# The remainder of v in an attention kernel: from one SBUF copy in one operation instead of from two PSUM banks in two

## The chip, the cores and the metric

One core of a Trainium2 chip runs the whole program. The metric is the device time of one execution in microseconds (us). The core has five engines that run their own instruction lists in order and wait for each other by semaphores: TensorE (PE; its weight loads are shown apart as PEld), VectorE (DVE), ScalarE (ACT), GpSimd (POOL) and SyncE (SP), which issues the DMAs. SBUF is the working memory; PSUM is the memory that matmuls write, in banks of 128 x 512 numbers of 32 bits.

## What is computed

A transformer block on x of 2048 tokens x 1024 features, modulated by a condition c. Cut to what matters here:

```python
# half A: attention with 32 heads of 32, in 4 segments of 512 tokens, with a memory (M, z)
h = layernorm(x) * (1 + ca) + sa
q, k, v = h @ wq, h @ wk, h @ wv              # per head, per segment s
p = softmax(q_s k_s^T * scale + causal mask)
a_dot = p @ v_s
a_mem = (phi(q_s) @ M) / (phi(q_s) @ z + 1e-6)
o = g * a_mem + (1 - g) * a_dot               # g = sigmoid(beta) per head
M, z = M + phi(k_s)^T v_s, z + sum(phi(k_s))
x = x + ga * (o @ wo)
# half B: token-mixing MLP
x = x + gb * (w2 gelu(w1 layernorm(x)^T * ... + b1) + b2)^T
```

The kernel reaches the precision of 32-bit numbers by splitting operands into parts of fewer bits. For v, the parts are three bf16 numbers: vp part 1 is v rounded to bf16, r1 = v - part 1 is the remainder, part 2 is r1 rounded to bf16, part 3 is r1 - part 2. The change is about where r1 is computed from.

## The kernel before, in words

**Stages.** Modulation and the first segment's normed tokens (to about 60 us of the run), attention (about 60 to 1085 us, its end overlapping the output projection "po"), and the MLP (L862 and its helpers) to the end.

**Attention.** Heads go in 8 groups of 4, segments in two passes of two; a round t of 32 is one group and one segment. A count n goes through the 128 heads of all rounds, and each step n does `scores(n)` (L475 to L490), `maxima(n+3)` (L440, L441, L447 to L450), `values(n-1)` (L504 to L521) and one of four pieces of `project` for the round two ahead:

- pieces 0 and 1 project k and v of half the segment's tokens into one bank of PSUM, tag "pj", of which there are two (nps, L196). ScalarE then copies from the bank: k to `k32` (L358), v to `v32` (L359, 32-bit, in SBUF), v rounded to bf16 to the first part of `vp` (L364). VectorE subtracts that part from the bank's v, into half of `r1` (L365 and L366).
- piece 2 transposes k into the next "pj" bank (kps, L372), splits it (L123 on ScalarE, L126 on VectorE), projects q into the one after (qps, L204), and splits that. It also makes phi(q) and phi(k) and starts the DMAs that stack the operands ("sk") of the scores.
- piece 3 rounds r1 into the second part of vp (L399, ScalarE), subtracts into the third (L400, VectorE), and reads and updates the memory (rd L412, up L422).

The two "pj" banks are taken in turn: first half of k and v, second half, kps, qps, and then the next round's first half. A bank is taken again when all readers of its tile have finished. `v32` and `r1` are single buffers, `vp` has three.

**Order.** Each engine runs its list in order. The lists are not simply the program's order: the framework plans them when the program is built, from its own durations and the dependencies of the tiles, so that on TensorE pieces of a projection stand between scores, maxima and values of other heads. `issue_after` adds a few orders by hand, none of them at the changed line.

**Other work in the stage.** GpSimd masks the exponentials (L486) and makes the second part of p (L490, two operations of 128 x 640 per head, reading and writing SBUF); VectorE takes the maxima (L441), the sums over parts (L507 to L511) and splits of weights (L126).

Of the kernel before, what the change touches and what calls it, by code (L numbers as in the profile page):

```python
# [12 lines left out]
ALU = mybir.AluOpType  # L13
# [32 lines left out]
def attention_and_mlp(ctx, tc, x, wq, wkv, wo, beta, w1, b1, w2, b2, c, wm_a, wm_b, out):  # L46
    nc = tc.nc
    V, A, G, T, SY = nc.vector, nc.scalar, nc.gpsimd, nc.tensor, nc.sync
# [17 lines left out]
    a = par.__enter__()  # L66
# [9 lines left out]
    def bank(tag, bufs, name):  # L76
        return psum.tile([P, 512], F32, tag=tag, bufs=bufs, name=name)
# [41 lines left out]
    def split(dst, src, hi_eng, lo_eng):  # L119

        hi, lo = dst[:, 0], dst[:, 1]
        if hi_eng is A:
            last_hi[0] = A.copy(hi, src)  # L123
        else:
            hi_eng.tensor_copy(hi, src)
        lo_eng.tensor_tensor(lo, src, hi.bitcast(F32), op=ALU.subtract)  # L126
# [62 lines left out]
    def kv_chunk(w, h, half, k, ps):  # L189
        wt = w["v", k // 2]  # L190
        o = 256 * (k % 2)
        n = 6 * k
        for i, j in ((0, 0), (0, 1), (1, 0)):
            for aa in range(2):
                tt = 2 * half + aa
                T.matmul(ps[:, aa], h[:, j, 128 * tt:128 * tt + 128], wt[:, i, o:o + 256],  # L196
                         start=(n == 0), stop=(n >= 6 * NK - 2), skip_group_check=True)
                n += 1

    def q_chunk(w, h, k, ps):  # L200
        wt = w["q", k // 4]
        o = 128 * (k % 4)
        for n, (i, j) in enumerate(((0, 0), (0, 1), (1, 0))):
            T.matmul(ps, wt[:, i, o:o + 128], h[:, j], start=(k + n == 0), stop=(3 * k + n == 3 * NK - 1))  # L204

    def two_tiles(ps):
        return ps.rearrange("p (a n) -> p a n", a=2)
# [51 lines left out]
    for i in range(2):  # L259
        ps = bank("pj", 2, f"scps{i}")  # L260
# [67 lines left out]
    def stack(t, h):  # L328


        sk = st[t]["sk", h] = skt[t % 2][h]
        skf = sk.bitcast(F32)
        src = st[t]["sg"].bitcast(F32)[32 * h:32 * h + 32]
        SY.dma_start(skf[0:32], src[:, 0:3:2])
        SY.dma_start(skf[32:64], src[:, 0:4:3])
        last_sk[t, h] = SY.dma_start(skf[64:96], src[:, 1:3])

    def project(t, piece):
        pr, g, seg = its[t]
        if piece == 0:  # L340
            st[t] = {}
        w = W[pr, g]
        hp = [hpages[seg, ct] for ct in range(NK)]
        d = st[t]
        if piece in (0, 1):
            if piece == 0:
                d["k32"] = pj.tile([P, 4, 128], F32, tag="k32", bufs=1, name=f"k32_{t}")
                d["v32"] = pj.tile([P, 4, 132], F32, tag="v32", bufs=1, name=f"v32_{t}")
                G.memset(d["v32"][:, :, 128:132], 1.0)
            half = piece  # L350
            k32, v32 = d["k32"], d["v32"]
            if t:
                ps = two_tiles(bank("pj", 2, f"nps{t}_{half}"))
                for k in range(NK):
                    kv_chunk(w, hp[k], half, k, ps)
            else:
                ps = two_tiles(first[half])
            A.copy(k32[:, 2 * half:2 * half + 2], ps[:, :, 0:128])  # L358
            A.copy(v32[:, 2 * half:2 * half + 2, 0:128], ps[:, :, 128:256])  # L359
            if half == 0:  # L360
                d["vp"] = b.tile([P, 4, 4, NV], BF16, tag="vp", bufs=3, name=f"vp{t}")
                G.memset(d["vp"][:, :, :, 0:1], 1.0)
                d["r1"] = pj.tile([P, 4, 4, 32], F32, tag="r1", bufs=1, name=f"r1_{t}")
            A.copy(d["vp"][:, 2 * half:2 * half + 2, :, 1:33], ps[:, :, 128:256].rearrange("p a (h e) -> p a h e", h=4))  # L364
            V.tensor_tensor(d["r1"][:, 2 * half:2 * half + 2], ps[:, :, 128:256].rearrange("p a (h e) -> p a h e", h=4),  # L365
                            d["vp"][:, 2 * half:2 * half + 2, :, 1:33], op=ALU.subtract)  # L366
        elif piece == 2:
            k32 = d["k32"]
            d["sg"] = sg = pj.tile([P, 4, L], F32R, tag="sg", bufs=1, name=f"sg{t}")
            ps = bank("pj", 2, f"kps{t}")  # L370
            for i in range(4):
                T.transpose(ps[:, 128 * i:128 * i + 128], k32[:, i], ident)  # L372
            split(sg[:, 2:4], ps, A, V)
            if t:
                ps = bank("pj", 2, f"qps{t}")
                for k in range(NK):
                    q_chunk(w, hp[k], k, ps)
            else:
                ps = first[2]
            split(sg[:, 0:2], ps, A, V)  # L380
            if seg:
                r = pj.tile([P, L], F32, tag="tmp", bufs=2, name=f"rq{t}")
                A.activation(r, ps, AF.Relu, scale=-1.0)
                A.activation(r, r, AF.Exp, scale=-1.0)
                d["pq"] = pj.tile([P, L], F32, tag="pq", bufs=1, name=f"pq{t}")
                V.scalar_tensor_tensor(d["pq"], ps, 0.0, r, op0=ALU.max, op1=ALU.add)
            if seg < 3:
                r = pj.tile([P, L], F32, tag="tmp", bufs=2, name=f"rk{t}")
                kf = k32.rearrange("p a n -> p (a n)")
                A.activation(r, kf, AF.Relu, scale=-1.0)  # L390
                A.activation(r, r, AF.Exp, scale=-1.0)
                d["pk"] = pj.tile([P, 4, 128], F32, tag="pk", bufs=1, name=f"pk{t}")
                V.scalar_tensor_tensor(d["pk"].rearrange("p a n -> p (a n)"), kf, 0.0, r, op0=ALU.max, op1=ALU.add)
            for h in range(3):
                stack(t, h)
        else:
            stack(t, 3)
            vp, r1 = d["vp"], d["r1"]
            A.copy(vp[:, :, :, 33:65], r1)  # L399
            V.tensor_tensor(vp[:, :, :, 65:97], r1, vp[:, :, :, 33:65], op=ALU.subtract)  # L400
            memory(t)

    def memory(t):
        pr, g, seg = its[t]
        d = st[t]
        d["am"] = am = b.tile([P, 4, 128], F32, tag="am", bufs=3, name=f"am{t}")
        if seg:
            for half in range(2):
                ps = bank("ms", 1, f"rd{t}_{half}")[:, 0:264].rearrange("p (a n) -> p a n", a=2)
                for aa in range(2):  # L410
                    i = 2 * half + aa
                    T.matmul(ps[:, aa], d["pq"][:, 128 * i:128 * i + 128], MZ[:, g], start=True, stop=True)  # L412
                rd = b.tile([P, 2, 4], F32, tag="rd", bufs=2, name=f"rdd{t}_{half}")
                V.tensor_scalar_add(rd, ps[:, :, 128:132], 1e-6)
                V.reciprocal(rd, rd)
                V.tensor_tensor(am[:, 2 * half:2 * half + 2].rearrange("p a (h e) -> p a h e", h=4),
                                ps[:, :, 0:128].rearrange("p a (h e) -> p a h e", h=4),
                                rd.unsqueeze(3).to_broadcast([P, 2, 4, 32]), op=ALU.mult)
        if seg < 3:
            ps = bank("ms", 1, f"up{t}")  # L420
            for i in range(4):
                T.matmul(ps[:, 0:132], d["pk"][:, i], d["v32"][:, i], start=(i == 0), stop=(i == 3))  # L422
            if seg == 0:
                V.tensor_tensor(MZ[:, g], ps[:, 0:132], bdg[:, g], op=ALU.mult)
            else:
                tm = b.tile([P, 132], F32, tag="tm", bufs=1, name=f"tm{t}")
                V.tensor_tensor(tm, ps[:, 0:132], bdg[:, g], op=ALU.mult)
                G.tensor_tensor(MZ[:, g], MZ[:, g], tm, op=ALU.add)
# [139 lines left out]
    def spread(dst, i):  # L568
        SY.dma_start(dst, bass.AP(tensor=modd.tensor, offset=modd.offset + D * i, ap=[[0, P], [1, D]]))

    project(0, 0)
    project(0, 1)
    with tc.issue_after(last_wm.ins):
        seg_load(1)
    project(0, 2)
    project(0, 3)
    seg_chunks(1, 0, 8)
# [505 lines left out]
```

## Time and profile before

| what | value |
|---|---|
| runs | 2258.55, 2255.84, 2258.07 us; median 2258.07 |
| profiled execution, first to last instruction (its span) | 2252.7 us |
| median of the runs above that span | 5.4 us |
| mean granted clock of TensorE | 0.993 |
| L364 (ScalarE's copy of v's first part), 64 times | 350 / 385 / 430 ns (min / median / max) |
| L399 (ScalarE, second part), 32 times | 612 / 634 / 702 ns |
| bytes moved by DMA | 423.06 MB, mean 188 GB/s |

The profile is of one execution, whose whole time is not given beside its span; what lies before the first and behind the last instruction is not in it. Line numbers (L365) are those of the kernel printed above. A row of a group gives its engine, operation, the tiles it writes and reads, the count, the busy time in us, the mean of one in ns, and the idle time just before it with what ended it. A row of a wait says who waited for whom, the total in us, how often, and the longest. A row of a window gives for each engine its busy time and its number of instructions in it, then TensorE's granted clock, the DMA engines' share and their rate. A wait for several semaphores is put down to the one that came last.

### The profile page before, as it was taken

Reading aid. Unit: us, or ns where it says so; the run is one execution under the profiler, and the core shown is the slowest. Engines: PE = TensorE matmul, PEld = TensorE weight load, DVE = VectorE, ACT = ScalarE, POOL = GpSimd, SP = SyncE. Lnnn points to the kernel's source line nnn. Section 1 sums busy time; section 2 is a strip of 40 time slices with the busy share of each in tenths; the row PEclk is TensorE's granted clock in tenths of the full one; section 3 lists DMA queues with packets and bytes.
Section 4 is the critical chain, followed back from the end, with each engine's and each line's share of the span. In section 5 each row is a group of like instructions: output and inputs, shape, how many; then the busy total and the mean of one; then the engine's idle time right before and its main releaser. Section 6 shows DMA issues by size and latency. Waiting matters only on the chain.

```text
span 2252.7 us, 38407 instructions
## 1 busy us (share of the span) xinstructions
PE 2202.4 (98%) x13802; PEld 1899.4 (84%) x13802; DVE 1667.2 (74%) x3810; ACT 1147.9 (51%) x2106; POOL 739.8 (33%) x847
## 2 busy tenths in 40 slices
PE   7999999999999999999999999999999999999999
PEld 6888898888988889988888888888888888888887
DVE  6686677766777677655758866788888887968787
ACT  6486677665666656655536633533334242424232
POOL 5165566655666766655001200033330000000000
PEclk9999999999999999999999999999999999999999
DMA  6655565687567566675654587645556541414134
GB/s 262 204 172 168 145 191 170 197 260 233 164 192 212 168 182 204 171 224 174 228 202 168 206 325 278 253 182 223 210 206 238 206 154 57 154 57 145 57 122 150
DMA packets 175186, 423.06 MB, mean 188 GB/s; under 512 B 17524, under 2 KB 71828, under 8 KB 166036
## 3 DMA queue, kind: packets, MB, share of 16 engines
q1 hardware_dynamic: 174996, 420.61, 57.0%
q8 instruction: 110, 1.80, 0.3%
q14 instruction: 80, 0.66, 0.1%
HBM read 244.62 MB, written 125.06 MB: 164 GB/s over the span
## 4 chain that ended last, share of the span: by engine, by line
PE 88%; ACT 3%; POOL 3%; DMA 3%; DVE 3%; issue 1%; SPq 0%; DVEq 0%; ACTq 0%; POOLq 0%
PE mx L862 47%; PE nps L196 13%; PE po L732 8%; PE qps L204 7%; PE pv L504 3%; POOL ph L490 1%; PE a L475 1%; PE sx L440 1%; PE sz L440 1%; PE rd L412 1%; PE a L478 1%; ACT ph L488 1%; PE a L482 1%; PE up L422 1%; DMA h<-hT 1%
## 5 line engine op out<-in xcount | busy, mean ns | idle before, releaser
L862 PE MATMUL mx<-bU,sp 128*128 128x512 f32 x2352 | 534.4, 389 | 0.9 <-DVE ac L869 0.9
L862 PEld LDWEIGHTS mx<-bU,sp 128*128 128x128 f32 x2352 | 441.2, 188 | 93.6 <-issue 1.3
L196 PE MATMUL nps<-wv,h 128*128 128x256 f32 x3072 | 435.5, 283 | 4.0 <-POOL h L126 3.9
L123 ACT CAST sp<-wr 128x384 fp32r<-128x384 f32 (+2 forms) x408 | 216.9, 545 | 430.0 <-PE mx L862 351.7
L862 PE MATMUL mx<-bA,sp 128*128 128x512 f32 x1764 | 430.5, 389 | 0.0
L490 POOL TENSOR_TENSOR ph<-p,ph 128x640 f16<-128x640 f32 x256 | 377.8, 1496 | 151.8 <-ACT ph L488 151.6
L196 PEld LDWEIGHTS nps<-wv,h 128*128 128x128 f32 x3072 | 403.2, 189 | 11.1 <-POOL h L126 5.1
L862 PEld LDWEIGHTS mx<-bA,sp 128*128 128x128 f32 x1764 | 331.1, 188 | 68.7
L126 DVE TENSOR_TENSOR sp<-wr,sp 128x384 fp32r<-128x384 f32 (+2 forms) x408 | 259.8, 647 | 30.2 <-ACT sp L123 30.0
L869 DVE TENSOR_TENSOR ac<-mx,ac 128x512 f32<-128x512 f32 x280 | 189.6, 685 | 84.4 <-PE mx L862 83.8
L204 PE MATMUL qps<-h,wq 128*128 128x512 f32 x768 | 200.0, 406 | 2.3 <-DVE pv L507 1.1
L488 ACT CAST ph<-p 128x1280 f16<-128x1280 f32 x128 | 161.1, 1259 | 45.7 <-POOL p L486 44.9
L732 PE MATMUL po<-wo,ots 128*128 128x512 f32 x768 | 180.3, 391 | 0.0
L441 DVE CUSTOM_DVE_ANT_0 sx<-sx,mask 128x128 f32<-128x128 f32 (+1 forms) x256 | 110.0, 430 | 92.9 <-PE sx L440 91.6
L204 PEld LDWEIGHTS qps<-h,wq 128*128 128x128 f32 x768 | 143.7, 194 | 31.6 <-issue 2.8
L732 PEld LDWEIGHTS po<-wo,ots 128*128 128x128 f32 x768 | 143.1, 188 | 29.0
L862 PE MATMUL mx<-bB,sp 128*128 128x512 f32 x588 | 163.9, 389 | 0.0
L486 POOL TENSOR_SCALAR_AFFINE_SELECT p<-p 128x256 f32<-128x256 f32 x256 | 119.5, 475 | 129.9 <-ACT p L479 62.8
L504 PE MATMUL pv<-vp,ph 128*128 128x97 bf16 (+1 forms) x2560 | 143.4, 202 | 1.6 <-DVE red L511 1.3
L504 PEld LDWEIGHTS <-ph 128*128 128x128 f16 x2560 | 114.9, 98 | 24.5 <-issue 11.6
L862 PEld LDWEIGHTS mx<-bB,sp 128*128 128x128 f32 x588 | 110.4, 188 | 22.9
L869 DVE TENSOR_TENSOR cc<-mx,cc 128x512 f32<-128x512 f32 x140 | 94.9, 684 | 37.7 <-PE mx L862 37.7
(200 smaller groups left out, 3204.1 us busy)
## 6 DMA issues: line engine op xcount, KB each, us to landing
sk<-sg SPq DMA_DIRECT2D x384, 128.0 KB
wr<-in_w_dram SPq DMA_DIRECT2D x28, 1024.0 KB
wr<-in_w_dram SPq DMA_DIRECT2D x32, 768.0 KB
bstu<-ucd SPq DMA_DIRECT2D x28, 768.0 KB
wsp<-wv SPq DMA_DIRECT2D x32, 512.0 KB
rawm<-in_wm_b_dram SPq DMA_DIRECT2D x32, 512.0 KB
wv<-wsp SPq DMA_DIRECT2D x32, 512.0 KB
pcd<-cc SPq DMA_DIRECT2D x14, 1024.0 KB
```

The costliest lines, as they stand in the source:

```text
L123: last_hi[0] = A.copy(hi, src)
L126: lo_eng.tensor_tensor(lo, src, hi.bitcast(F32), op=ALU.subtract)
L196: T.matmul(ps[:, aa], h[:, j, 128 * tt:128 * tt + 128], wt[:, i, o:o + 256], start=(n == 0), stop=(n >= 6 * NK - 2), skip_group_check=True)
L204: T.matmul(ps, wt[:, i, o:o + 128], h[:, j], start=(k + n == 0), stop=(3 * k + n == 3 * NK - 1))
L441: marks[4 * t + h - LEADS, "V"] = V.tensor_tensor_reduce(o, o, mask[:, 384 - 128 * i:], 1.0, -3.0e38, op0=ALU.add, op1=ALU.max, accum_out= ...
L486: G.affine_select(w, w, pattern=[[0, 2], [1, 128]], compare_op=ALU.is_ge, fill=0.0, base=0, channel_multiplier=-1)
L488: marks[n, "A"] = A.copy(ph[:, 0], p32)
L490: marks[n, "G"] = G.tensor_tensor(ph[:, 1, c], p32[:, c], ph[:, 0, c], op=ALU.subtract)
L504: T.matmul(pv[:, i, 0:w], ph[:, part, o:o + 128], d["vp"][:, j, h, 0:w], start=(n == 0), stop=(n == 19), skip_group_check=True)
L732: T.matmul(ps, os_[:, i, P * ct:P * ct + P], wop[ct, nh][:, j], start=(n == 0), stop=(n == 3 * NK - 1))
L862: T.matmul(ps, ops[q][:, i, P * k:P * k + P], b[:, j], start=(m == 0 and first), stop=(m == 3 * nk - 1), skip_group_check=True)
L869: V.tensor_tensor(d, ps, d, op=ALU.add)
```

## The change

The two subtractions of 128 x 256 (one per half, each from the half's bank in PSUM, when its vp copy is done) are replaced by one of 128 x 512 behind the second half's copies. It reads v from `v32`, ScalarE's 32-bit copy in SBUF, and the first part from `vp`, also in SBUF, and writes r1 as before. The numbers computed are the same.

```diff
             A.copy(d["vp"][:, 2 * half:2 * half + 2, :, 1:33], ps[:, :, 128:256].rearrange("p a (h e) -> p a h e", h=4))
-            V.tensor_tensor(d["r1"][:, 2 * half:2 * half + 2], ps[:, :, 128:256].rearrange("p a (h e) -> p a h e", h=4),
-                            d["vp"][:, 2 * half:2 * half + 2, :, 1:33], op=ALU.subtract)
+            if half:
+                V.tensor_tensor(d["r1"], v32[:, :, 0:128].rearrange("p a (h e) -> p a h e", h=4), d["vp"][:, :, :, 1:33],
+                                op=ALU.subtract)
```

## The prediction

> **What bounds the kernel now.** I read the page first, then the stretches of the run (busy time of each engine by window), then TensorE's own waits in the stage that the change touches, then the rows of the changed line and of its nearest relatives, and last the timeline around two stalls. The page and the stretches:
>
> ```profile
> span 2252.7 us, 38407 instructions
> PE 2202.4 (98%) x13802; PEld 1899.4 (84%) x13802; DVE 1667.2 (74%) x3810; ACT 1147.9 (51%) x2106; POOL 739.8 (33%) x847
> ...
> core 0: us, PE busy (x) PEld busy (x) DVE busy (x) ACT busy (x) POOL busy (x), PEclk, DMA share, GB/s
> ...
> 60.00:1085.00 1025.00, 996.01 (x8426) 898.58 (x8426) 704.76 (x2109) 651.65 (x1186) 606.47 (x720) 0.99 0.64 191
> 1085.00:1150.00 65.00, 65.00 (x289) 53.81 (x288) 55.92 (x141) 41.68 (x80) 0.00 (x0) 1.00 0.70 227
> 1150.00:2252.70 1102.70, 1098.22 (x4842) 908.13 (x4840) 868.89 (x1464) 415.60 (x769) 99.27 (x64) 1.00 0.50 180
> ```
>
> TensorE bounds everything. In the attention stage (60 to 1085 us) it is busy for 996.0 of 1025.0 us, so 29.0 us is all that any change of waits could win there; behind it TensorE is busy without a pause (65.00 of 65.00 us), so what is won or lost in the stage moves the end by as much. VectorE at 705 us, ScalarE at 652 and GpSimd at 606 of 1025 are not the bound, but they decide when TensorE may go on. What it waits for in that stage:
>
> ```profile
> PE a L475 <- DMA sk<-nt: 4.7, 5, 2.5
> PE sx L440 <- DVE mx L441: 3.6, 7, 0.8
> PE a L475 <- ACT vp L364: 3.1, 2, 2.2
> PE kps L372 <- DVE r L365: 2.6, 3, 1.5
> PE sx L440 <- DVE mv L133: 2.4, 1, 2.4
> PE sy L440 <- DVE mx L441: 2.1, 7, 0.4
> ...
> PE qps L204 <- DVE pv L507: 1.1, 1, 1.1
> PE qps L204 <- DVE r L365: 1.1, 1, 1.1
> ```
>
> (Columns: total us, times, longest.) The changed line, L365, is named twice: 2.6 us in which the transposes of k (kps, L372) waited for it, and 1.1 us in which the projection of q (qps, L204) did. The reason is the pair of "pj" banks: kps takes the bank of the first half of k and v, qps that of the second, and a bank is free only when its last reader is done. That reader is now VectorE's subtraction.
>
> How much idle time lies under this hold is shown by two sets of windows, 31 each, one per project call but the first: from the start of the last k/v matmul to the start of the first qps matmul, and from the end of the second vp copy (L364) to the end of the second subtraction.
>
> ```profile
> 74.62:76.47 1.85, 1.84 (x11) 1.14 (x10) 1.25 (x6) 1.53 (x5) 0.00 (x0) 1.00 0.97 244
> ...
> 975.12:978.01 2.89, 2.89 (x32) 2.77 (x32) 1.60 (x6) 2.69 (x7) 2.81 (x4) 1.00 0.32 68
> sum 133.48, PE 111.46 PEld 90.55 DVE 111.78 ACT 110.20 POOL 93.54; mean PE 3.60 PEld 2.92 DVE 3.61 ACT 3.55 POOL 3.02
> ...
> 75.87:76.33 0.46, 0.46 (x2) 0.19 (x1) 0.46 (x4) 0.46 (x2) 0.00 (x0) 1.00 0.87 232
> ...
> 976.71:977.17 0.46, 0.46 (x10) 0.45 (x8) 0.42 (x1) 0.46 (x3) 0.46 (x2) 1.00 0.02 4
> sum 40.06, PE 30.88 PEld 23.86 DVE 38.89 ACT 27.07 POOL 26.62; mean PE 1.00 PEld 0.77 DVE 1.25 ACT 0.87 POOL 0.86
> ```
>
> The first sum: of TensorE's 29.0 idle us, 133.48 - 111.46 = 22.0 lie in the short spells between the k/v projection and the q projection, when its bulk work is held back. The second: the hold by the second subtraction alone is 40.06 us (1.29 us per call, though the operation takes 0.42), and TensorE is idle for 40.06 - 30.88 = 9.2 us of it. The rest of the 22.0 us has other owners (the wait for L364, for the maxima at L441, for the first subtraction).
>
> **The change part by part.** The rows of what goes, of its nearest relative, and of the neighbours:
>
> ```profile
> L365 DVE TENSOR_TENSOR r<-nps,vp x64: 395/419/426, 54.0 to 976.7; 128x256 f32<-128x256 f32 x64
> ...
> L400 DVE TENSOR_TENSOR vp<-r,vp 128x512 bf16<-128x512 f32 x32 | 31.6, 988 | 1.6 <-ACT vp L399 1.4
> ...
> L400 DVE TENSOR_TENSOR vp<-r,vp x32: 630/692/1898, 58.0 to 978.7; 128x512 bf16<-128x512 f32 x32
> ...
> L490 POOL TENSOR_TENSOR ph<-p,ph x256: 1396/1412/2443, 111.8 to 1061.9; 128x640 f16<-128x640 f32 x128
> ...
> ACT vp L399 <- DVE r L365: 1.2, 3, 0.6
> ...
> ACT p L476 <- POOL ph L490: 14.0, 9, 2.6
> ```
>
> *Removed: 64 subtractions of 256 columns.* 64 x 0.419 = 26.8 us of VectorE, and with them the hold on both banks. After the change the last reader of each bank is ScalarE's vp copy, which exists already and which the subtraction waited for. The new wait of kps and qps is therefore never later than the old one by their own data.
>
> *Added: 32 subtractions of 512 columns, both inputs in SBUF.* The trace of before does not have it. L400 is the nearest row: the same engine, width and pair of inputs (one f32, one bf16 in runs of 32 out of 97), only the output is bf16 there and f32 here. Its shortest is 0.630 us and its longest 1.898; 32 at the mean 0.988 are 31.6 us, so VectorE gains between 26.8 - 32 x 0.630 = 6.6 us and loses 32 x 1.898 - 26.8 = 33.9 us. I take the mean, a loss of 31.6 - 26.8 = 4.8 us, 0.7% of its 705 us in the stage; as VectorE is idle for 320 us of the stage, I cost the busy time itself at nothing. If that cover were gone (a maximum queued right behind it), the 5.7 us of TensorE's waits for L441 (3.6 + 2.1) would grow.
>
> Why L400 is spread by a factor of three while L365 never leaves 395 to 426 ns: GpSimd's subtraction L490 runs beside it, and L490 itself goes from 1.396 up to 2.443 us. [...]
>
> *Moved: the first half's subtraction, to behind the second half's copies.* No DMA and no GpSimd instruction moves with it, and SP's queue is untouched. v32, a single buffer, gets one more reader, but its next writer is the next call's L359, a round later (1025 us over 32 rounds are 32 us). What waits for the result is L399 on ScalarE (third part of v) and then L400; the finished vp is used two rounds later, so only ScalarE's queue behind L399 matters: exponentials of L476 to L483, the splits of kps and qps. Now L399 waited only 1.2 us for L365. If the new operation ends later by 0.988 - 0.419 = 0.57 us, 32 calls are 18.2 us at most that ScalarE stands still; ScalarE is idle for 373 us of the stage, so I let 1.5 us of it come through to TensorE (from nothing to 18.2; that little because only three L399 waited so far).
>
> *Gained.* Two stalls, from VectorE's and TensorE's timelines:
>
> ```profile
> 442.48 1.42 DVE L126 TENSOR_TENSOR wv<-rawv,wv 128x512 fp32r<-128x512 f32 x1
> 443.82 0.41 DVE L365 TENSOR_TENSOR r<-nps,vp 128x256 f32<-128x256 f32 x1
> ...
> 444.29 0.66 PE L372 MATMUL kps<-ident,k 128*128 128x128 f32 x4 [1.49 <-DVE r L365]
> ...
> 543.91 0.42 DVE L365 TENSOR_TENSOR r<-nps,vp 128x256 f32<-128x256 f32 x1
> ...
> 544.48 0.70 PE L204 MATMUL qps<-h,wq 128*128 128x512 f32 x2 [1.13 <-DVE pv L507]
> ```
>
> In the first, the subtraction sat in VectorE's queue behind a weight split and TensorE stood for 1.49 us. In the second the wait is put down to L507, but the subtraction ended at 544.33 and qps started 0.15 us later: this 1.1 us belongs to L365 as well. So with today's order, 2.6 + 1.1 + 1.1 = 4.8 us are owed to it directly; that is the lower bound if nothing else is late. The upper one is the 9.2 us of the second sum, if the freed projection work fills every hole under the hold. I take 7.0, the middle. What is late next is the vp copy itself (the 3.1 us of L364 stay) and the maxima. Gain 7.0 less 1.5 given back: 5.5 us.
>
> **Sum.** Span 2252.7 - 5.5 = 2247.2. The runs' median, 2258.07, is 5.4 above the profiled span; with the same 5.4 around it the forecast is 2252.6 us, 0.24% less. About 0.2%, 4.5 us, is what a measurement of this kernel can tell from no change, so this is just beyond it.
>
> **The rivals.**
>
> *A. The hold goes, the idle time stays.* TensorE runs its list in order, and between projections the list holds scores, maxima and values with waits of their own. Then only the 4.8 us are won and most is given back at the next wait. For it: the largest single waits of the stage (4.7 for nt's DMA, 3.1 for L364) are not the subtraction's. Against: 22 of 29 us lie exactly where projection work is held back. Time: within 4.5 us of 2258.07; say 2257.
>
> *B. Slower, by GpSimd's subtraction beside the new one.* Place: VectorE's new operation meets a running L490, waits for it, L399 behind it blocks ScalarE, and with it the exponentials that TensorE and GpSimd live on; L490 is lengthened in turn, and L476 already waits 14.0 us for it. Price: 0.57 us per call at L400's mean, 18.2 us in all, and 32 x (1.898 - 0.419) = 47 us at its longest. It cancels the 7.0 us when 0.22 us per call reaches TensorE, and is slower by over 0.2% from (7.0 + 4.5) / 32 = 0.36 us per call, two thirds of the mean. With all of the 18.2 us through: 2258.07 - 7.0 + 18.2 = 2269; with three quarters, 2264.7. For it: POOL is busy for 606 of 1025 us, so most new operations will meet it. Against: L400, which meets it today, keeps nobody waiting on TensorE.
>
> *C. The order of the work changes.* The streams are interleaved by a planner when the program is built; other durations give other orders in the whole stage. A stage with a third more of its 29.0 us idle, or a third less, is 9.7 us either way: 2268 or 2248. Nothing in the profile says which; that few holes are left makes more idle time the likelier.
>
> That the change does not do what it says could only be if another reader held the banks; L358, L359 and L364 remain, all on ScalarE and ahead of the removed one, so I give this nothing.
>
> **How the numbers follow.** Forecast (a saving of 4.5 to 15 us): 0.40; A: 0.22; B: 0.25; C: 0.13, of which 0.09 slower and 0.04 faster. So faster 0.44, same 0.22, slower 0.34. The forecast's own range is 2243 to 2253.5: its lower end is the 9.2 us with nearly half of the other 12.8 us of holes and nothing given back, its upper end the 0.2% bound. The whole range must reach to B: 2243 to 2268, which leaves out the last part of B and C and the deepest savings.
>
> **What would show it.** Right: kps and qps no longer wait for r, the time from the second vp copy to the first qps matmul shrinks by about a microsecond per call, TensorE's idle time in the stage falls from 29.0 to about 23.5 us. The new subtraction's row should look like L400's, with a mean near 0.99 us and a longest near 1.9. B shows as a longer wait of L399 for r and of L476 for L490. C shows as waits that moved between lines that have nothing to do with v. Wrong: idle time of TensorE at or above 29 us, or a median above 2262.6.

## The result

| kernel | runs | median, us | ratio to before, 95% interval |
|---|---|---|---|
| before | 16 | 2256.94 | |
| changed | 16 | 2253.44 | 0.9978 [0.9971, 0.9985] |
| changed, second series (before: 2257.22) | 11 | 2253.73 | 0.9995 [0.9985, 1.0005] |
| changed, third series (before: 2256.17) | 12 | 2253.40 | 0.9991 [0.9979, 1.0003] |

The changed kernel is a little faster: by 3.5, 3.5 and 2.8 us of medians. The ratios on record are not the quotients of these medians (those are 0.9984, 0.9985 and 0.9988): by them it is 0.22% faster in the first comparison and 0.05 to 0.09% in two later ones, whose intervals reach no change. Its profiled execution has a span of 2247.2 us, which is the forecast span to the tenth; that is luck, since this execution has the highest granted clock of its 16 runs (0.998; their mean is 0.9954). The page of the changed kernel, and the attention stage as a window (a line of the code behind the change stands one line lower than before, so L366 is the new subtraction, L400 and L401 the two that follow it):

```profile
span 2247.2 us, 38365 instructions
PE 2195.4 (98%) x13802; PEld 1892.9 (84%) x13802; DVE 1671.5 (74%) x3778; ACT 1145.6 (51%) x2106; POOL 748.6 (33%) x847
...
60.00:1085.00 1025.00, 994.70 (x8452) 897.22 (x8452) 712.18 (x2091) 651.06 (x1191) 615.10 (x720) 1.00 0.64 191
```

TensorE's idle time in the stage is 1025.00 - 994.70 = 30.3 us; before it was 29.0. What fell is its busy time over the whole run, 2202.4 to 2195.4 us, although it executes the same 13802 matmuls. Its waits in the stage (total us, times, longest):

```profile
PE a L476 <- DMA sk<-nt: 5.4, 4, 2.1
PE sx L441 <- DVE mx L442: 5.1, 12, 1.2
PE sz L441 <- DVE mx L442: 3.3, 7, 1.3
PE sy L441 <- DVE mx L442: 3.0, 6, 0.7
PE pv L505 <- DVE red L512: 2.8, 2, 1.5
PE pv L505 <- POOL ph L491: 2.1, 2, 1.2
...
PE kps L373 <- ACT k L358: 0.8, 3, 0.3
...
PE kps L373 <- ACT vp L364: 0.6, 3, 0.3
```

No matmul waits for the subtraction any more. In its place the waits of sx, sy and sz for VectorE's maxima are 5.1 + 3.0 + 3.3 = 11.4 us, where they had 3.6 + 2.1 + 0.6 = 6.3. The same windows as in the prediction, summed over 31 calls, from the last k/v matmul to the first qps matmul; and below it the sums from the end of the second vp copy to the first qps matmul, the first of the changed kernel and the second of the kernel before:

```profile
sum 108.20, PE 92.30 PEld 74.53 DVE 88.66 ACT 93.34 POOL 66.99; mean PE 2.98 PEld 2.40 DVE 2.86 ACT 3.01 POOL 2.16
...
sum 19.99, PE 16.96 PEld 15.79 DVE 16.32 ACT 15.74 POOL 12.73; mean PE 0.55 PEld 0.51 DVE 0.53 ACT 0.51 POOL 0.41
```

```profile
sum 60.25, PE 49.55 PEld 40.06 DVE 54.63 ACT 45.21 POOL 40.28; mean PE 1.60 PEld 1.29 DVE 1.76 ACT 1.46 POOL 1.30
```

The q projection starts (60.25 - 19.99) / 31 = 1.3 us earlier after the last copy, and the idle time in the spell falls from 22.0 to 108.20 - 92.30 = 15.9 us. These 6.1 us are what the forecast meant; but 7.4 us of idle time appeared elsewhere in the stage. What makes this execution faster all the same is TensorE's granted clock (the first number behind the busy times). All stretches at half clock that start in the stage, before and after:

```profile
193.69:200.51 6.82, 6.22 (x37) 5.37 (x38) 5.09 (x16) 2.76 (x8) 2.01 (x3) 0.50 0.50 193
258.54:265.37 6.83, 6.39 (x16) 4.90 (x17) 4.84 (x19) 4.00 (x6) 3.42 (x3) 0.50 0.39 152
415.55:418.97 3.42, 3.42 (x10) 2.64 (x9) 2.11 (x6) 1.84 (x3) 2.38 (x3) 0.50 0.78 210
476.99:483.82 6.83, 6.08 (x41) 5.17 (x39) 6.47 (x22) 3.98 (x7) 3.83 (x7) 0.50 0.96 317
545.26:548.67 3.41, 3.41 (x10) 2.63 (x9) 2.52 (x6) 0.00 (x0) 1.72 (x2) 0.50 0.88 321
```

```profile
129.06:132.47 3.41, 3.41 (x22) 2.90 (x20) 1.70 (x9) 2.89 (x9) 0.84 (x2) 0.50 0.78 278
327.03:330.44 3.41, 3.41 (x22) 3.20 (x21) 3.35 (x6) 2.63 (x6) 3.41 (x3) 0.50 0.54 114
```

Before, 27.3 us of the stage ran at half clock, after, 6.8 us. Half of the 20.5 us between them, 10 us, is what that can cost a TensorE that is always busy, by an estimate from the granted 0.50, and more than the two spans differ by (5.5 us); in the one case measured below, 3.41 us at half clock cost 1.7. It is not always that large: the profiled executions of the changed kernel in the second and third series have 10.2 and 13.7 us at half clock. Two of the stretches follow idle time visibly: the one at 258.54 begins while TensorE stands for 2.43 us (put down to mv, L133), the one at 415.55 right behind the 1.05 us for L365. Each run lists its clock, and a line fitted to the changed kernel's 16 runs (0.993 to 0.998) falls by 1.4 us per 0.001. The kernel before has 0.9925 in the mean of the 22 runs of the second series (the first lists it for the changed kernel alone), the changed one 0.9954 and, in the second series, 0.9950: by that line 3.5 to 4 us, all of the gain. At a clock of 0.994 the kernel before takes 2254.3 us (three runs), the changed one 2254.1 to 2255.2 (two runs of the first series). Fitted with one slope of the clock for both kernels, the runs of the second series put the changed kernel 1.3 us (plus or minus 1.9) above the kernel before at equal clock, those of the third 2.1 (1.4). So as planned it is not faster at equal clock, and it ran at a higher one.

### The profile page after: what moved, and what is told of

The parts are those of the page before. It is cut to its first block, busy times and chain, and to the rows that moved or that the text cites. A ratio compares the mean times of both kernels' runs of the same rounds, so it can differ in the third digit from the quotient of the medians.

```text
span 2247.2 us, 38365 instructions
## 1 busy us (share of the span) xinstructions
PE 2195.4 (98%) x13802; PEld 1892.9 (84%) x13802; DVE 1671.5 (74%) x3778; ACT 1145.6 (51%) x2106; POOL 748.6 (33%) x847
## 4 chain that ended last, share of the span: by engine, by line
PE 83%; DVE 7%; DMA 3%; POOL 2%; ACT 2%; issue 2%; SPq 1%; ACTq 0%; DVEq 0%; POOLq 0%
PE mx L863 44%; PE nps L196 11%; PE po L733 8%; PE qps L204 7%; PE pv L505 3%; PE a L476 1%; PE sx L441 1%; PE sz L441 1%; POOL ph L491 1%; DMA wr<-in_w_dram 1%; DVE ac L870 1%; PE a L479 1%; PE rd L413 1%; PE a L483 1%; PE sy L441 1%
## 5 line engine op out<-in xcount | busy, mean ns | idle before, releaser
L196 PE MATMUL nps<-wv,h 128*128 128x256 f32 x3072 | 441.7, 284 | 4.7 <-POOL h L126 3.8
L491 POOL TENSOR_TENSOR ph<-p,ph 128x640 f16<-128x640 f32 x256 | 378.5, 1499 | 170.2 <-ACT ph L489 169.6
L126 DVE TENSOR_TENSOR sp<-wr,sp 128x384 fp32r<-128x384 f32 (+2 forms) x408 | 260.1, 648 | 31.5 <-ACT sp L123 31.3
L487 POOL TENSOR_SCALAR_AFFINE_SELECT p<-p 128x256 f32<-128x256 f32 x256 | 131.7, 524 | 108.4 <-ACT p L484 54.8
L204 PEld LDWEIGHTS qps<-h,wq 128*128 128x128 f32 x768 | 140.9, 189 | 26.8 <-ACT vp L364 0.3
```

Source lines behind the costliest of these rows:

```text
L487: G.affine_select(w, w, pattern=[[0, 2], [1, 128]], compare_op=ALU.is_ge, fill=0.0, base=0, channel_multiplier=-1)
L491: marks[n, "G"] = G.tensor_tensor(ph[:, 1, c], p32[:, c], ph[:, 0, c], op=ALU.subtract)
```

## Experiments

Three theories. **Banks**: the forecast's; the freed banks save TensorE's waits. **Order**: the gain comes from the order in which the work was planned anew. **Contention**: rival B; the new operation costs VectorE, ScalarE and GpSimd what the banks save. To part them, each engine's list as planned for one kernel was written out and imposed on another, by edges that order two instructions of an engine without a wait:

```diff
         attention_and_mlp(ctx, tc, **args)
+        hold_order(tc, nc)    # the list of each engine, from a table
```

**The new subtraction in the old order.** The changed kernel with the lists of the kernel before.

> The changed kernel's subtraction (one of 512 columns from SBUF, both banks freed by ScalarE), but every engine's list held in the order of the kernel before; the new subtraction stands where the second of the old ones stood. Freed banks (the forecast's theory): kps and qps no longer wait for r, so the 4.8 us of waits owed to it go, less about 1: 3 to 5 us faster than before (ratio 0.9978 to 0.9987), TensorE's idle time in the stage about 25 us. Order (rival): the gain of the changed kernel lies in its other order of the work, so here the time is that of before within 1.5 us (0.9993 to 1.0007). Contention (rival B): the longer subtraction holds ScalarE, slower by 2 us or more.

Measured: 2250.45 us (6 runs) against 2257.22, ratio 0.9974 [0.9962, 0.9985]. The longest waits of TensorE in the stage:

```profile
PE a L476 <- DMA sk<-nt: 10.4, 9, 4.1
PE sx L441 <- DVE mx L442: 3.4, 7, 0.8
PE sx L441 <- DVE mv L133: 2.4, 1, 2.4
PE sy L441 <- DVE mx L442: 2.2, 7, 0.4
```

And the stage as a window:

```profile
60.00:1085.00 1025.00, 996.54 (x8439) 900.23 (x8437) 715.74 (x2091) 655.19 (x1191) 613.70 (x720) 0.99 0.64 191
```

With the order unchanged, the waits of kps and qps for r are gone, nothing took their place at the maxima, and the kernel is about 6 us faster than before, beyond the expected range and more than the changed kernel in its own order. Its clock is 0.9937 in the mean, 0.0012 above that of before: 1.7 us by the line above. At 0.994 its four runs have a mean of 2250.1 us, 4.2 under the three of before. That waits save these 4.2 us is inferred from the runs; the profiled execution does not show it. Its idle time in the stage is 28.5 us, not the expected 25 or so, because the waits for the DMA of sk rose from 4.7 to 10.4 us, which takes back what kps and qps gained; why they rose was not tried. Order alone cannot make this gain, and contention does not eat it.

**Again, beside the changed kernel.**

> The changed kernel's subtraction in the order of the kernel before, a second time (0.9974 the first): 0.9968 to 0.998 if the first was no accident. At or above 0.999 if the saving in this order was chance, and then the freed banks would be worth nothing that can be measured.

> The changed kernel a third time (0.9978 and 0.9995 so far), beside the next one, to price its own planned order. If the other order costs nothing, both have the same ratio within 0.0007. If it eats a part of what the freed banks give, this one is 1 to 4 us slower than the next: 0.998 to 0.9993.

Measured: 0.9976 [0.9965, 0.9988] (12 runs, 2249.52 us) and, for the changed kernel, 0.9991 [0.9979, 1.0003]. The saving in the old order is no accident; in its profiled execution the idle time in the stage is 27.1 us. The newly planned order eats half of the saving or more: 3.9 us between the medians, though the two intervals overlap.

**The old subtractions in the new order.** The kernel before with the lists of the changed kernel; its 64 subtractions find their own places.

> The kernel before's two subtractions from the banks, but every engine's list held in the order of the changed kernel; only the two subtractions find their own place in VectorE's list. Freed banks: this order was planned for banks that come free early; held by VectorE they come late, so kps and qps wait again and the time is at or above that of before (ratio 0.999 to 1.003). Order: the time is that of the changed kernel, 3 to 6 us under before (0.9973 to 0.9987).

Measured: 2286.43 us, ratio 1.0134 [1.0117, 1.0151], far beyond what either theory said.

```profile
PE kps L372 <- DVE r L365: 21.0, 19, 3.1
PE pv L504 <- DVE red L511: 4.3, 3, 2.7
PE qps L204 <- DVE r L365: 4.1, 9, 1.4
```

The new order puts kps and qps where only an early bank lets them run: held by VectorE they wait 25.1 us instead of 3.7, and the clock falls to 0.9902. Part of this may be the places that the planner then found for the two subtractions. The new order without the freed banks is no gain; it is a bet on them.

**The banks freed, but two subtractions.** In the old order, with only the source changed:

```diff
-            V.tensor_tensor(d["r1"][:, 2 * half:2 * half + 2], ps[:, :, 128:256].rearrange("p a (h e) -> p a h e", h=4),
+            V.tensor_tensor(d["r1"][:, 2 * half:2 * half + 2],
+                            v32[:, 2 * half:2 * half + 2, 0:128].rearrange("p a (h e) -> p a h e", h=4),
```

> Two subtractions of 256 columns as before, in the order of the kernel before on every engine, but each reads v from the copy in SBUF: the banks are freed by ScalarE, nothing else changes. Freed banks: 3 to 5 us faster than before, as with the one operation (0.9978 to 0.9987). Order: the time of before within 1.5 us. Contention: two inputs in SBUF stretch each subtraction beyond the 395 to 426 ns of before, up to about 1.9 us, with the waits of GpSimd's subtraction a little longer.

Measured: 1.0006 [0.9996, 1.0017], 2258.56 us. No matmul waits for r here either, and nothing is won: what the theory of the banks expected did not come. The group of the two subtractions here, then that of the one (new subtraction in the old order); busy us and mean ns behind the bar:

```profile
L365 DVE TENSOR_TENSOR r<-v,vp 128x256 f32<-128x256 f32 x64 | 46.6, 733 | 8.6 <-ACT vp L364 8.5
```

```profile
L366 DVE TENSOR_TENSOR r<-v,vp 128x512 f32<-128x512 f32 x32 | 31.3, 978 | 3.5 <-ACT vp L364 3.4
```

A subtraction of 256 columns takes 733 ns from SBUF in the mean and took 418 from the bank, with single ones up to 1641. The trace shows whom it meets: 48 of the 64 overlap an operation of GpSimd and take 837 ns in the mean, the other 16 take 406 to 426 as from the bank. Of the 32 wide ones, 26 overlap one and take 1045 in the mean, the other 6 take 673 to 692. From the bank, 48 of the 64 overlapped GpSimd too and none was longer than 426. So the contention is with GpSimd, and one operation meets it about half as often as two. With 26.8 us before, the two are 19.8 us more of VectorE, against 4.5 for the one, and the maxima behind them come later (3.4 us of waits of sx with the one):

```profile
PE sx L441 <- DVE mx L442: 6.0, 10, 1.2
```

GpSimd's L491 goes from a mean of 1496 ns to 1510 (1513 with the one operation). That the 20 us are the whole cause of the lost gain was argued from these rows, not tried by itself.

**The new subtraction, the banks held.** In the old order, with VectorE reading one column of each bank where the old subtractions stood:

```diff
+            V.tensor_copy(d["r1"][:, 2 * half, 0, 0:1], ps[:, 0, 128:129])
+            if half:
+                V.tensor_tensor(d["r1"], v32[:, :, 0:128].rearrange("p a (h e) -> p a h e", h=4), ...)
```

> The order of the kernel before on every engine and the changed kernel's one subtraction of 512 columns from SBUF, but VectorE still reads one column of each bank where the two old subtractions stood, so the banks are held as long as before. Freed banks: with the hold back, kps and qps wait for VectorE again and the gain of the same order without the hold (ratio 0.9974) is lost: 2256 to 2261 us (0.9995 to 1.002), with about 4 us of waits of kps and qps for the column reads. If instead the gain lay in the shorter work of VectorE (one operation for two), the ratio stays at 0.997 to 0.998.

Measured: 0.9994 [0.9984, 1.0004], 2254.87 us (12 runs).

```profile
PE kps L374 <- DVE r L365: 1.9, 3, 1.2
PE qps L204 <- DVE r L365: 1.7, 2, 0.9
PE sx L442 <- DVE r L365: 1.5, 2, 0.7
```

Here L365 is the column read. With the hold back, kps and qps wait 3.6 us again, and most of the gain is gone: the ratio rises by 0.2% over the same order without the hold. It is 0.0001 under the expected range and the median 1.1 us under; by medians 3.2 of the 6.8 us are left, so a part of the gain may be the one operation instead of two. This run also adds 64 small operations (153 ns each), 9.4 us of VectorE, so a part of the loss may be theirs (sx waits 1.5 us for them).

**Another order without the change, and with it.** Two independent lines exchanged, which makes the planner order the work anew:

```diff
-            A.copy(k32[:, 2 * half:2 * half + 2], ps[:, :, 0:128])
             A.copy(v32[:, 2 * half:2 * half + 2, 0:128], ps[:, :, 128:256])
+            A.copy(k32[:, 2 * half:2 * half + 2], ps[:, :, 0:128])
```

> The kernel before with two independent lines exchanged (v is copied out of the bank ahead of k, on ScalarE); it computes and waits for the same, and only the planned order differs: 2065 of 13578 matmuls have another one ahead of them. If the order decides more than the change, the time moves by over 0.2% (about 4.5 us) either way; if orders are worth little, it stays within 0.1% of before (0.999 to 1.001).

> The changed kernel with the same two lines exchanged; again another planned order (2164 matmuls have another one ahead of them than in the changed kernel). Freed banks: as fast as the changed kernel and faster than the kernel before with the lines exchanged, by 3 to 6 us. Order: anywhere within 15 us of before, without regard to its partner.

Measured: 1.0004 [0.9995, 1.0014] for the kernel before, 0.9982 [0.9973, 0.9990] for the changed one. The other order alone does not move the time, and the partner with the changed subtraction is the faster one by 4.3 us of medians, as the theory of the banks expected. But the hold that it should have freed is hardly there in the first of the two; this is the only wait of kps or qps for r in its stage:

```profile
PE kps L372 <- DVE r L365: 0.2, 1, 0.2
```

So these 4.3 us are not the waits that the forecast counted, and what makes them stays open. The kernel before with the lines exchanged also has a clock of 0.9946, against 0.9920 without: this planned order has a higher clock and the same time (2258.09 us against 2258.11), with no bank freed; its waits for the DMA of sk are 8.8 us, 4.7 before, and those of sx for the maxima 5.8, 3.6 before.

**The changed kernel beside these.**

> The changed kernel itself, beside the others on the same chip: ratio 0.997 to 0.9985 by its first measurement. Clock: if the gain is fewer stretches at half the TensorE clock, its runs show a mean granted clock above that of before's runs by 0.001 to 0.003, and runs of either kernel at the same clock take the same time within 2 us; if it is fewer or shorter waits, the spans differ by 4 to 5 us at equal clock.

Measured: 0.9995 [0.9985, 1.0005], outside the expected range, with a clock of 0.9950 against 0.9925, as the theory of the clock expected. At equal clock the spans do not differ by 4 us, as said above: as it was planned, the changed kernel's gain goes with the clock. Single runs at one listed clock are up to 4 us apart (2248.92 and 2253.09 us at 0.998), so this rests on the means; and what gave it the higher clock was not shown.

**One stall less.** In the old order with the new subtraction, near 257 us: VectorE's two weight splits (L126, 2.65 us) behind three maxima, not ahead of them.

```diff
-L126 TensorTensor wv   (two, ahead of L442 sx)
 L442 sx 128, L442 sy 256, L366 r, L442 sx 384
+L126 TensorTensor wv   (two)
```

> The changed kernel's subtraction in the order of the kernel before, with one thing moved: in the eighth round VectorE's two weight splits, which keep TensorE waiting for 2.43 us near 257 us of the run, stand behind three maxima instead of ahead of them. Clock: that stall is followed by a stretch of 3.4 to 6.8 us at half the TensorE clock, so taking the stall away gives its 2.4 us and 1.7 to 3.4 us of clock: 4 to 6 us under the run without the move (2250.45 there), ratio to before 0.9948 to 0.9957, mean granted clock up by 0.001. Waits alone: 2.4 us (0.9963). The wait moves on to the next maximum or to the splits' readers: no change (0.9974).

Measured: 2245.27 us, ratio 0.9948 [0.9936, 0.9961]. TensorE at that place, without the move and with it:

```profile
254.19 0.33 PE L483 MATMUL a<-sk 98*128 98x256 f32 x1
256.96 0.44 PE L441 MATMUL sx<-sk 96*128 96x384 f32 x1 [2.43 <-DVE mv L133]
```

```profile
254.46 0.33 PE L483 MATMUL a<-sk 98*128 98x256 f32 x1
254.84 0.44 PE L441 MATMUL sx<-sk 96*128 96x384 f32 x1
```

The idle 2.43 us are gone, and so is the stretch of 3.41 us at half clock behind them; matched matmul by matmul, the trace with the move gains 4.0 us at this place, 2.4 by idle time and 1.7 by the clock. Over the whole stage both executions have 23.9 us at half clock, since a later stretch is 10.24 us long here and 6.83 there; the mean clock of the runs is 0.0011 higher. It is the fastest version here, 12.8 us of medians under the kernel before (2258.11 in that series).

## Why the prediction was right

The sign and the size hold. The reason holds in the runs with the order held; in the kernel as planned it does not carry the gain, so that the number came out is in good part luck. The time also lies at the forecast's edge: 2253.44 us is 4.6 under the 2258.07 from which the forecast started, where 4.5 parted it from rival A, and 3.5 under the median of all 16 runs.

- *The hold on the banks costs TensorE about 5 us.* Right in size: 4.2 us at equal clock with the order unchanged, where 5.5 was forecast (7.0 gained, 1.5 given back), and most of the gain goes when the hold comes back. The second stall was read rightly: the wait of qps that the trace put down to L507 is gone as well. But banks freed with two operations gain nothing, so the hold alone is not the whole account.
- *The new subtraction looks like L400.* Right: mean 925 ns and longest 1885 in the changed kernel, 0.988 us and 1.9 forecast. In the trace of the kernel before, the 21 of L400's 32 that overlap an operation of GpSimd take 1151 ns in the mean, the other 11 take 630 to 690. That one operation is cheap where two are not was not seen: the prediction priced only the one, and in the old order two lose all that the banks give.
- *ScalarE's L399 would stand still for up to 18.2 us, of which 1.5 come through.* This copy (L400 in the changed kernel; it makes the second part of v, not the third, as the prediction calls it) waits 7.7 us for r, 1.2 before, so the bound holds; how much of it reaches TensorE was not measured by itself.
- *TensorE's idle time in the stage falls to 23.5 us.* **This step failed.** It is 30.3 us, and the prediction itself had named 29 or more as a sign of being wrong. The spell between the projections lost 6.1 us of idle time, and the rest of the stage gained 7.4. Rival C, given 0.13 and priced at 9.7 us either way, came true beside the forecast: the planned order eats half or more of the saving.
- *Not in the sum at all: the clock.* In the one case tried, a stall cost TensorE its own 2.4 us and 1.7 more by the half clock behind it. The changed kernel's runs have a higher clock, worth 3.5 to 4 us by the line above, and at equal clock it is not faster as planned.
- *The 5.4 us around the span.* Wrong: the listed run with the span 2247.2 took 2248.92, so 1.7 us lie around it. The other 3.7 were the profiled execution of the kernel before, which was one of its faster ones (2252.7 + 1.7 is 2254.4, with a median of 2256.94). With 1.7 the forecast span would have meant 2248.9 us.

Rival A, the hold goes and the idle time stays, describes the changed kernel's trace: the maxima took over. By the median of 16 runs its time, within 4.5 us of before, fits too; only with the order held is the saving larger than A allows. Rival B's mechanism is there (of the two subtractions from SBUF those that overlap GpSimd take 837 ns in the mean, the others 406 to 426), and with them the kernel has none of the gain: 2258.56 us against 2257.22.

## What to carry to other kernels

Ask which engine is the last reader of a PSUM bank that TensorE needs next, and try that reader on a copy in SBUF; then count how often the moved operation will meet GpSimd (here 26 of 32 times done once, 48 of 64 in two pieces), and do it once, not in pieces. A planner that orders the work anew hides a change of this size, so hold the order to measure the change, and look for single stalls of 2 us in the order itself: one of them was worth as much as the change.

## What the runs showed of the hardware

The stretches at half clock in the traces here are 3.41 or 6.83 us long (10.24 twice, in the run with one stall less and in the second one of the new subtraction in the old order). In three traces they start whole multiples of 3.41 us apart: the five of the kernel before 19, 46, 18 and 20 of them, the two of the changed kernel 58, and the five of the new subtraction in the old order (at 193.15, 258.00, 380.88, 473.04 and 531.07 us) 19, 36, 27 and 17. The 3.41 us ahead of the third stretch of the kernel before:

```profile
412.14:415.55 3.41, 2.04 (x21) 1.56 (x21) 3.41 (x10) 3.41 (x10) 3.31 (x2) 1.00 1.10 346
```

The 3.41 us ahead of the second stretch of the changed kernel, and two such lengths of it that no stretch followed:

```profile
323.62:327.03 3.41, 2.41 (x10) 1.32 (x11) 3.05 (x14) 3.41 (x7) 0.89 (x3) 1.00 0.55 159
760.52:763.93 3.41, 2.69 (x34) 2.41 (x33) 3.08 (x13) 1.62 (x5) 3.13 (x3) 1.00 0.96 369
763.93:767.35 3.42, 1.82 (x26) 1.70 (x27) 1.02 (x4) 1.44 (x4) 1.23 (x5) 1.00 0.03 11
```

So 1.4 and 1.0 us of idle time in 3.41 us were followed by half clock, and 1.6 us were not; what decides stays open. (Idle is what the profile does not count as busy.)
